# Block-sparse attention and an MLP mixer on one core: the mask product in two pieces, relayouts on VectorE alone, another order of the same work

## The chip, the cores and the metric

The kernel runs on one core of one Trainium2 chip. The metric is the device time of one execution in microseconds (us). A run takes the median of several executions; the profile is of one execution, whose span (first to last instruction) is a little shorter than its time. Engines: PE (TensorE), ACT (ScalarE), DVE (VectorE), POOL (GpSimd) and SP (SyncE), which here issues DMAs and passes on events.

## The reference, cut to what matters

```python
B, H, S, D = 4, 8, 768, 64                        # q, k, v: float32
mask = (|blk_i - blk_j| <= 1) | first or last block row or column
       | three sampled blocks of 32 for each block row
scores = where(mask, q @ k^T / sqrt(D), -1e9)
attn = exp(scores - max) / sum
x = (attn @ v), heads side by side                # [4, 768, 512]
h = relu(x^T @ w_tok1) @ w_tok2                   # token mixer, 768 -> 256 -> 768
u = x + h^T
out = u + relu(u @ w_ch1) @ w_ch2                 # channel mixer, 512 -> 1536 -> 512
```

## The kernel before, in words

All matmuls are bfloat16 with float32 sums in the eight PSUM banks (`banks`). The 32 heads are worked in 16 pairs p. A pair's 768 queries fall into three thirds t, its 768 keys into three pieces jj; a step (p, t, jj) makes the scores of 256 keys by 256 queries for both heads: four matmuls into two banks (`scores`, L917). ACT takes the exponential of the 1,024 columns into the tile `et` of the third (L930). For the first four pairs the mask is part of the scores' matmul (88 rows in place of 64). From pair 4 on (NT0 = 4) the scores use 64 rows, so that the two heads run at once on the two halves of PE's rows, and DVE multiplies `et` by the 0/1 tile `mask` (the function `cut` in `scores`, L948). `CUTS`, chosen by `BASE["cuts"]`, says for which pieces jj one product stands: before, (0, 1, 2) in one operation, which can run when all three exps of the third are done. Then the values product follows (L1086 in full rows for the first pairs, then `pv_halves` by L375), a reciprocal (L1099 and L1040) and a division (L1100 and L1041) into the tile `x`.

Q, K and V come by loads that POOL issues. `relayout` (L757 to L780) copies them into the order that the transposes and the values product take: `klay` and `qlay` (L765) and `vaug` (L762). Before, for pairs from `ra` = 5 on such a copy may go to DVE or ACT. K and Q are transposed by PE for pairs under 8 and by DMA transposes that SP issues from pair 8 on (`crossbar`, L788). The mixer of a batch follows when its four pairs are done: the token mixer (`tok`, `tok_halves`; relus at L1128, L1130, L1218, L1220, additions at L1264, L1326, L1385), the transposes of u (L1145 by SP, L1165 by PE for batch 1) with their evacuations (L1176, L1420, L1449), and the channel mixer `ch` with its relus (L1128 on ACT, L1130 on DVE) and the final addition and store (L1567, L1572 for 1,024 columns; L1615, L1626 for 512).

From pair 4 to the end of the attention PE works in halves (`halves`): each product is split over the two halves of the contraction's rows, so that two matmuls run at once. [...]

The order of the instructions on every engine is fixed when the program is built. A planner (`Planner`) steps through an estimated time. Every piece of work is entered with an estimated cost, with the events it waits for and with a priority; whenever an engine is free in the plan, the ready piece of lowest priority number is emitted next. `P.op` takes work for DVE, ACT or SP; `P.stream` takes PE's work. If a piece may go to two engines, the one that is free first in the plan gets it. The priorities, some limits of PSUM banks (`cps`, `cpo`, `cpm`, `cch`) and some margins (`jit`, `m1`, `m2`, `grace`, `shift`) are read through `KN`: a table `BASE`, and over it `BY_TIME`, which gives other values in numbered stretches of the plan, each 5,000 ns long (`Knobs.stretch`). All costs in these lines are the planner's own, in ns; they decide the order alone.

Of the kernel before, what the change touches and what calls it, by code (L numbers as in the profile page):

```python
# [20 lines left out]
BY_TIME = {  # L21
    0: dict(cch=2),
    1: dict(norm=2.3, m2=300.0, tokp=0.7, ev2=2.0, cch=3),
    2: dict(m2=450.0, ev2=0.9, cpo=1),
    3: dict(norm=2.3, m2=300.0, tokp=0.7, ev2=2.0, cch=3, cpm=3, shift=6000.0, add=0.3, grace=100.0, ev4=1.2),
    5: dict(norm=2.3, m2=150.0, tokp=0.7, ev2=2.0, cch=3, cpm=3, shift=6000.0, add=0.3, grace=100.0, ev4=1.2, cps2=3, relayk=2.0, cut=0.7),
    6: dict(fin=4.1, cps=3, trp=1.6),
    7: dict(fin=4.1, cps=3, trp=1.6),
    8: dict(fin=4.1, cps=3, trp=1.6, add=0.3, back=1.1, cut=0.5),
    9: dict(shift=6000.0),  # L30
    10: dict(fin=4.1, cps=3, trp=1.6, add=0.3, back=1.1, cut=0.5, m2=300.0, ev2=0.9, jit=300.0),
    12: dict(fin=4.1, cps=3, trp=1.6, add=0.3, back=1.1, cut=0.5, m2=300.0, ev2=0.9, jit=300.0, tokp=1.7, backp=0.9, cpo=2, m1=0.0),
    13: dict(fin=4.1, cps=3, trp=1.6, add=0.3, back=1.1, cut=0.5, m2=300.0, ev2=0.9, jit=2000.0, tokp=1.7, backp=0.9, cpo=2, m1=0.0, late=3.5, relayk=0.8),
    14: dict(m2=0.0, cch=2, m1=0.0, cut=6.0, ev4=1.2),
    16: dict(add=0.3, late=1.05, cch=2, ev4=2.0, relayk=3.5),
    17: dict(m1=0.0, back=1.1, add=0.95),
    18: dict(m1=0.0, back=1.1, add=0.95, cut=1.1, m2=300.0, cpo=2),
    19: dict(cps2=3, toks=0.4, jit=300.0, relayv=3.0, relayk=3.5),
    20: dict(m1=0.0, back=1.1, add=0.95, cut=1.1, m2=0.0, cpo=2, toks=-0.5, backp=0.45, cpm=1),
    21: dict(m1=0.0, back=1.1, add=0.95, cut=1.1, m2=0.0, cpo=2, toks=-0.5, backp=0.45, cpm=1),  # L40
    22: dict(m1=100.0, back=1.1, add=0.95, cut=6.0, m2=0.0, cpo=2, toks=-0.5, backp=0.45, cpm=1, relayk=0.8),
    23: dict(m1=100.0, back=1.1, add=0.95, cut=6.0, m2=0.0, cpo=2, toks=-0.5, backp=0.45, cpm=1, relayk=0.8, jit=300.0, cps=3),
    24: dict(m1=100.0, back=1.1, add=0.95, cut=6.0, m2=0.0, cpo=2, toks=-0.5, backp=0.45, cpm=1, relayk=0.8, jit=300.0, cps=3),
    25: dict(jit=450.0, cps2=2, relayv=4.6),
    27: dict(jit=450.0, cps2=2, relayv=4.6, cps=2, backp=0.45, cpo=2, relu=0.85),
    28: dict(jit=450.0, cps2=2, relayv=4.6, cps=2, backp=0.45, cpo=2, relu=0.85),
    29: dict(jit=450.0, cps2=2, relayv=4.6, cps=2, backp=0.45, cpo=2, relu=0.85, toks=0.4, relayk=4.5),
    30: dict(jit=450.0, cps2=2, relayv=4.6, cps=2, backp=0.45, cpo=1, relu=0.85, norm=0.6, cpm=2, backt=0.9),
    31: dict(back=1.1, cpm=1, jit=1300.0),
    32: dict(jit=450.0, cps2=2, relayv=4.6, cps=2, backp=0.45, cpo=1, relu=0.85, norm=1.0, cpm=2, backt=0.9, m1=100.0, shift=0.0),  # L50
    33: dict(tokp=0.7, cps=3, ev4=1.2, shift=-6000.0, cch=2),
    34: dict(chs=0.8, m1=100.0, ev2=1.2, cpo=2, backt=0.2),
    35: dict(jit=0.0, cpo=2, chs=1.1),
}


# [238 lines left out]
def kernel(  # L295
# [12 lines left out]
    nc = tc.nc  # L308
# [7 lines left out]
    NV = 4  # L316
# [15 lines left out]
    vaug = [sb1.tile([128, 2, NC, 66], BF16, name=f"vaug{n}") for n in range(NV)]  # L332
# [32 lines left out]
    def halves(n, cost, outs, lhs, rhs, deps, tags, begin, done, prio, ahead=0.0):  # L365
# [25 lines left out]
        for x in range(n):  # L391
# [11 lines left out]
    P = Planner(  # L403
        {"et": NET, "a_t": 2, "o": 3, "rc": 2, "uT": 2},
# [3 lines left out]
    )  # L408
# [106 lines left out]
    def ind_part(lo, n):  # L515
# [14 lines left out]
        out=ident[:, :], in_=free(one[:, 0:1], 0, [[0, 128]]), compare_op=ALU.is_equal, fill=0.0,  # L530
# [19 lines left out]
    for res, val, lo, hi, op in (  # L550
# [3 lines left out]
            out=res[R, :], in0=val[R, :], scalar1=lo, scalar2=hi, op0=ALU.max, op1=ALU.min  # L554
# [3 lines left out]
        out=bandneg[R, :], in0=notband[R, :], scalar1=inner[R, 0:1], scalar2=MASKVAL,  # L558
# [5 lines left out]
        out=differ[R, :, :], in0=free(kbi[R, 0:1], 0, [[1, 24], [0, 3]]),  # L564
# [188 lines left out]
    def relayout(p):  # L753
        lays = {}
        for nm in ("k", "q", "v") if p >= NT0 else ("v",):
            raw = raws.pop((nm, p))
            arr = arrive.pop((nm, p))  # L757

            def emit(eng, nm=nm, raw=raw):
                copy = nc.scalar.copy if eng == "act" else nc.vector.tensor_copy  # L760
                if nm == "v":
                    copy(out=vaug[p % NV][:, :, :, 0:64], in_=raw)  # L762
                else:
                    lay = sbw.tile([128, NC, 2, D], BF16, tag=f"{nm}lay", bufs=2, name=f"{nm}lay{p}")
# [12 lines left out]
            lays[nm + "ev"] = P.op(("dve", "act") if p >= BASE["ra"] else ("dve",), {"dve": 320.0, "act": 735.0}, deps, emit,  # L777
                                  prio="relayk" if nm != "v" else "relayv")
            copied[nm, p] = lays[nm + "ev"]
        va_there[p] = lays["vev"]  # L780
        return lays

    def crossbar(p):

        lays = relayout(p)
        for nm, bufs, there in (("k", ktb, kT_there), ("q", qtb, qT_there)):
            def emit(eng, nm=nm, bufs=bufs):
                nc.sync.dma_start_transpose(  # L788
                    out=bufs[p % NV][:, 0, :].rearrange("e (c s) -> e c s", c=NC),
                    in_=lays[nm][:, :, :, :].rearrange("p c h d -> p (c h d)"),  # L790
                )
            deps = [lays[nm + "ev"], qk_done[p - NV]]
            ev = P.op(("sp",), {"sp": 1300.0}, deps, emit, prio=1, lat=5000.0)
            there[p, 0], there[p, 1] = ev, ev

    def transposes(p):
# [4 lines left out]
        if p == 0:  # L801
            relayout(p)
            for nm in ("k", "q"):
                copied[nm, p] = Ev(START)
            for hd in range(2):
                kT_there[p, hd], qT_there[p, hd] = k_first[1], q_first[2]
            yield from first_rest()
            return
        for hd in range(2):
            kT_there[p, hd], qT_there[p, hd] = Ev(), Ev()  # L810
        lays = relayout(p)
        for nm, bufs, there in (("k", ktb, kT_there), ("q", qtb, qT_there)):
            box, last, rel = {}, Ev(), Ev()
# [934 lines left out]
```

## Time and profile before

| | |
|---|---|
| median of 3 runs (lowest to highest) | 245.05 us (244.9 to 245.28) |
| profiled execution: time, span | 245.05 us, 243.4 us |
| granted clock of TensorE, mean | 0.999 |
| exps L930 on ACT | 144 of 1,025 ns, 141.6 us |
| mask products L948 on DVE | 36 of 1,703 ns, 61.3 us |
| relayouts L762 and L765 on ACT | 3, of 823, 824 and 833 ns |
| relayouts L762 and L765 on DVE | 37, by form 352 to 476 ns |
| fences L361 | 16 on SP (45.2 to 69.4 us), 73 on POOL (71.1 to 199.5 us) |
| crossbar issues L788 on SP | 16, medians 1.22 and 1.28 us, landing after 2.8 to 4.4 us |
| mixer transposes L1145 on SP | 5, median 1.44 us, landing after 3.7 to 4.7 us |

A group's line in the profile gives the line of the code, the engine, the operation, what it writes and reads with shapes, and the count; then its busy time, the mean time of one, and the idle time of the engine just before, with what ended it. A line of the waits gives who waited, for whom, the time in total, how many times and the longest. Matmuls are pipelined, so that their busy times overlap; the times between their starts tell more.

### The profile page before, as it was taken

How to read it: one execution, taken by the hardware profiler on the slowest of the kernel's cores; microseconds unless marked ns; L12 is line 12 of the kernel's file. 1: busy time of each engine (PE TensorE's matmuls, PEld its weight loads, DVE VectorE, ACT ScalarE, POOL GpSimd, SP SyncE). 2: the span in 40 equal slices, each digit the busy share in tenths (PEclk: the TensorE clock that was granted, in tenths of full speed). 3: DMA queues.
4: the chain of work that ended last, by engine and by line, in shares of the span. 5: the costliest groups of instructions: out<-in, count | busy, mean ns of one | idle time of the engine just before them, and what ended most of it. 6: DMA issues, size and time to landing. Idle time of an engine off the chain costs nothing.

```text
span 243.4 us, 9647 instructions
## 1 busy us (share of the span) xinstructions
PE 237.0 (97%) x4343; PEld 170.9 (70%) x4343; DVE 172.1 (71%) x285; ACT 170.0 (70%) x187; POOL 49.5 (20%) x86
## 2 busy tenths in 40 slices
PE   7999999999999999999999999999999999999994
PEld 3689999767777677867878667677688664565444
DVE  5975987979899889799789788987687535100222
ACT  6889999868797699788778987798658400366000
POOL 8966987357710000000000000000000000000000
PEclk9999999999999999999999999999999999999999
DMA  7999999999993874131207270501030024200132
GB/s 163 166 214 203 209 207 203 206 201 196 201 180 76 132 167 137 38 118 33 40 3 89 46 155 3 154 25 67 3 67 3 5 89 127 112 3 0 43 132 86
DMA packets 39755, 26.17 MB, mean 108 GB/s; under 512 B 21985, under 2 KB 37105, under 8 KB 39713
## 3 DMA queue, kind: packets, MB, share of 16 engines
q0 software_dynamic: 15104, 12.98, 33.9%
q1 hardware_dynamic: 24064, 12.17, 20.4%
q8 instruction: 34, 0.56, 0.9%
q10 hardware_dynamic: 544, 0.39, 0.6%
q14 instruction: 9, 0.07, 0.1%
HBM read 26.74 MB, written 6.29 MB: 136 GB/s over the span
## 4 chain that ended last, share of the span: by engine, by line
PE 89%; DMA 3%; ACT 3%; POOL 2%; DVE 1%; issue 0%; POOLq 0%; DVEq 0%; ACTq 0%
PE banks L375 53%; PE banks L917 14%; PE banks L1601 9%; PE banks L1536 6%; DMA kraw<-in_k_dram 3%; ACT et L930 3%; PE banks L1086 3%; PE banks L858 1%; PE banks L1354 1%; DVE et L948 1%; POOL vraw L447 1%; PE banks L1296 1%; PE banks L1376 1%; PE banks L1318 1%; POOL ktb L517 0%
## 5 line engine op out<-in xcount | busy, mean ns | idle before, releaser
L930 ACT ACTIVATE et<-banks 128x1024 bf16<-128x1024 f32 x144 | 141.6, 1025 | 28.3 <-PE banks L917 24.5
L948 DVE TENSOR_TENSOR et<-et,mask 128x2976 bf16<-128x2976 bf16 x36 | 61.3, 1703 | 8.3 <-ACT et L930 8.2
L917 PE MATMUL banks<-qtb,ktb 64*128 64x256 bf16 (+1 forms) x576 | 63.7, 270 | 0.7 <-ACT et L930 0.2
L375 PE MATMUL banks<-uT,w_ch 64*128 64x512 bf16 (+1 forms) x576 | 60.6, 322 | 0.0
L375 PE MATMUL banks<-w_ch,rc 64*128 64x512 bf16 x384 | 54.3, 376 | 0.0
L375 PEld LDWEIGHTS <-et 64*128 64x128 bf16 x1728 | 39.2, 94 | 9.4 <-POOLq L361 3.0
L917 PEld LDWEIGHTS <-ktb 64*128 64x128 bf16 (+1 forms) x576 | 33.8, 94 | 15.1 <-issue 1.4
L375 PE MATMUL banks<-vaug,et 64*128 64x65 bf16 x1728 | 42.0, 190 | 0.2 <-issue 0.2
L375 PEld LDWEIGHTS <-w_ch 64*128 64x128 bf16 x576 | 28.6, 94 | 8.4 <-SPq L361 0.6
L1128 ACT ACTIVATE rc<-banks 128x512 bf16<-128x512 f32 (+1 forms) x28 | 21.0, 749 | 17.0 <-PE banks L1536 15.0
L1615 DVE TENSOR_TENSOR o<-banks,x 128x512 f32<-128x512 f32 x7 | 4.8, 692 | 28.2 <-PE banks L1601 28.2
L1130 DVE TENSOR_SCALAR rc<-banks 128x1024 bf16<-128x1024 f32 x17 | 20.8, 1221 | 3.4 <-PE banks L375 3.2
L375 PEld LDWEIGHTS <-rc 64*128 64x128 bf16 x384 | 17.3, 94 | 7.9 <-POOLq L361 0.5
L1601 PE MATMUL banks<-w_ch,rc 128*128 128x512 bf16 (+2 forms) x120 | 21.3, 337 | 0.0
L1601 PEld LDWEIGHTS <-rc 128*128 128x128 bf16 x120 | 10.7, 98 | 10.6 <-issue 0.8
L375 PEld LDWEIGHTS <-w_tok 64*128 64x128 bf16 x288 | 14.5, 109 | 3.3 <-POOLq L361 0.6
L1041 DVE TENSOR_TENSOR x<-banks,recip 128x256 bf16<-128x256 f32 x36 | 15.3, 425 | 1.2
L1536 PE MATMUL banks<-uT,w_ch 128*128 128x512 bf16 (+1 forms) x96 | 15.8, 326 | 0.0
L1536 PEld LDWEIGHTS <-w_ch 128*128 128x128 bf16 x96 | 9.4, 98 | 6.4
L1567 DVE TENSOR_TENSOR o<-banks,x 128x1024 f32<-128x1024 f32 x8 | 9.8, 1224 | 5.1 <-PE banks L375 5.0
L1086 PE MATMUL banks<-vaug,et 128*128 128x65 bf16 x288 | 13.1, 193 | 0.0
L1264 DVE TENSOR_TENSOR x<-banks,x 128x512 bf16<-128x512 f32 (+2 forms) x12 | 10.3, 887 | 2.9 <-PE banks L375 2.7
(122 smaller groups left out, 198.0 us busy)
## 6 DMA issues: line engine op xcount, KB each, us to landing
out_dram<-o SPq DMA_DIRECT2D x8, 512.0 KB, 3.6
w_ch<-in_moe_w_ch_dram POOLq DMA_DIRECT2D x8, 384.0 KB, 9.8
vraw<-in_v_dram POOLq DMA_DIRECT2D x10, 192.0 KB, 7.9
out_dram<-o SPq DMA_DIRECT2D x7, 256.0 KB, 2.0
kraw<-in_k_dram POOLq DMA_DIRECT2D x9, 192.0 KB, 9.2
qraw<-in_q_dram POOLq DMA_DIRECT2D x9, 192.0 KB, 8.3
w_tok<-in_moe_w_tok_dram POOLq DMA_DIRECT2D x2, 384.0 KB, 10.0
qf<-in_v_dram POOLq DMA_DIRECT2D x4, 192.0 KB, 7.8
```

Source lines behind the costliest of these rows:

```text
L375: mms.append(nc.tensor.matmul(out=outs()[o](x), lhsT=lhs(o, x, r), rhs=rhs(o, x, r), start=(back == 0 and x == 0), stop=(back == 1 and x = ...
L917: nc.tensor.matmul(out=ps[:, hd, 256 * i : 256 * i + 256], lhsT=ktb[n][rows, h, 256 * jj + 128 * i : 256 * jj + 128 * i + 128], rhs=qtb[n] ...
L930: nc.scalar.activation(out=ets[p, t][:, jj, :, :, :].rearrange("k i h q -> k h i q"), in_=ps.rearrange("k h (i q) -> k h i q", i=2), func= ...
L948: nc.vector.tensor_tensor(out=et, in0=et, in1=free(mask[:, 2 * lo, 256 * t + EDGE : 256 * t + EDGE + 1], 0, [[S, 2 * n], [0, 2], [1, w]]), ...
L1041: nc.vector.tensor_tensor(out=free(xs[b][:, pb // 2, 2 * t, 128 * (pb % 2) : 128 * (pb % 2) + 128], 0, [[64, 2], [256, 2], [1, 64]],), in0 ...
L1086: nc.tensor.matmul(out=po[:, hd, c, :], lhsT=et[:, jj, i, hd, 128 * c : 128 * c + 128], rhs=va[:, hd, 2 * jj + i, 0:65], start=(jj == 0 an ...
L1128: nc.scalar.activation(out=o(), in_=src(), func=AF.Relu)
L1130: nc.vector.tensor_scalar(out=o(), in0=src(), scalar1=0.0, scalar2=None, op0=ALU.max)
L1264: nc.vector.tensor_tensor(out=u, in0=src, in1=u, op=ALU.add)
L1536: nc.tensor.matmul(out=in_bank(pbox["pm"], [k, 128 * n])[:, x // 4, :], lhsT=w_ch1[:, x % 4, 128 * cc : 128 * cc + 128], rhs=st[b]["uT"][: ...
L1567: nc.vector.tensor_tensor(out=t[:, :, :].rearrange("p c (g e) -> p g c e", g=2), in0=free(banks[:, pbox["pm"][0], :], 0, [[256, 2], [512, ...
L1601: nc.tensor.matmul(out=pbox["pm"][:, 0:n], lhsT=box["rc"][:, cc, 128 * sc : 128 * sc + 128], rhs=w_ch2[:, cc, lo : lo + n], start=(cc == 0 ...
```

## The change

`cuts` goes from 2 to 1: a third's mask product becomes two operations, one of the pieces jj = 0 and 1 (8 x 248 = 1,984 elements of each partition) and one of jj = 2 (992). Relayouts may go to DVE alone, and `ra` is gone. The table `BY_TIME` is another one, so that the planner gives another order of the work on PE, DVE, ACT and SP; POOL's loads keep theirs. The stretch length, the code of `crossbar` and all other planned costs are the same in both programs. The core of the diff:

```diff
-    norm=0.6, add=0.3, ev2=1.2, ev4=3.3, grace=0.0, m1=100.0, m2=150.0, nt0=4, cuts=2, xbar=8,
+    norm=0.6, add=0.3, ev2=1.2, ev4=3.3, grace=0.0, m1=100.0, m2=150.0, nt0=4, cuts=1, xbar=8,
...
-    backp=0.45, backt=0.3, turn=[1], ra=5,
+    backp=0.45, backt=0.3, turn=[1],
 }
 BY_TIME = {
-    0: dict(cch=2),
-    1: dict(norm=2.3, m2=300.0, tokp=0.7, ev2=2.0, cch=3),
-    2: dict(m2=450.0, ev2=0.9, cpo=1),
...
-    35: dict(jit=0.0, cpo=2, chs=1.1),
+    1: dict(backt=0.3, chs=1.1, m2=450.0, cpm=3, cps=3),
+    2: dict(relayv=3.0, ev4=2.0, m1=200.0, grace=0.0, fin=0.9),
...
+    35: dict(m1=0.0, shift=1500.0, relayk=6.0, back=0.9, m2=450.0),
 }
...
             def emit(eng, nm=nm, raw=raw):
-                copy = nc.scalar.copy if eng == "act" else nc.vector.tensor_copy
                 if nm == "v":
-                    copy(out=vaug[p % NV][:, :, :, 0:64], in_=raw)
+                    nc.vector.tensor_copy(out=vaug[p % NV][:, :, :, 0:64], in_=raw)
                 else:
                     lay = sbw.tile([128, NC, 2, D], BF16, tag=f"{nm}lay", bufs=2, name=f"{nm}lay{p}")
-                    copy(
+                    nc.vector.tensor_copy(
                         out=lay[:, :, :, :], in_=raw.rearrange("p h c d -> p c h d")
                     )
...
-            lays[nm + "ev"] = P.op(("dve", "act") if p >= BASE["ra"] else ("dve",), {"dve": 320.0, "act": 735.0}, deps, emit,
+            lays[nm + "ev"] = P.op(("dve",), {"dve": 320.0}, deps, emit,
                                   prio="relayk" if nm != "v" else "relayv")
```

What follows from it in the built programs, by counting instructions (before, after): mask products 36 of 2,976, then 36 of 1,984 and 36 of 992; relayouts on ACT 3, then 0, and on DVE 37, then 40; relus of 1,024 columns on DVE (L1130) 17, then 13, and on ACT (L1128) 10, then 14; token relus on DVE (L1220) 3, then 5, and on ACT (L1218) 3, then 1; one evacuation L1420 goes from DVE to ACT; output additions L1567 8, then 7, and L1615 7, then 9; fences 89, then 88. PE's matmuls do the same products, with pair 6's Q turned in halves and a third of batch 2's second channel layer in full rows in place of halves.

More of the change, by code (lines that the diff above doesn't have):

```diff
@@ L20 @@
 )
 BY_TIME = {
-    0: dict(cch=2),
-    1: dict(norm=2.3, m2=300.0, tokp=0.7, ev2=2.0, cch=3),
-    2: dict(m2=450.0, ev2=0.9, cpo=1),
[L25 to L52, printed above, removed]
-    35: dict(jit=0.0, cpo=2, chs=1.1),
+    1: dict(backt=0.3, chs=1.1, m2=450.0, cpm=3, cps=3),
+    2: dict(relayv=3.0, ev4=2.0, m1=200.0, grace=0.0, fin=0.9),
+    3: dict(relayv=3.0, ev4=2.0, m1=200.0, grace=0.0, fin=0.9),
@@ new lines @@
+    4: dict(relayv=3.0, ev4=2.0, m1=200.0, grace=0.0, fin=0.9, cpo=2, cch=2, relu=5.5, add=0.3, trp=0.8),
+    6: dict(relayv=3.0, ev4=2.0, m1=100.0, grace=0.0, fin=0.9, cpo=2, cch=2, relu=5.5, add=0.3, trp=0.8, cpm=2, ev2=1.2),
+    8: dict(relayv=3.0, ev4=2.0, m1=100.0, grace=0.0, fin=0.9, cpo=2, cch=2, relu=5.5, add=0.3, trp=0.8, cpm=2, ev2=1.2, cut=1.1, chs=4.0, relayk=2.0),
+    10: dict(m1=100.0, cpm=2, jit=450.0, cpo=1, late=1.05),
+    11: dict(ev2=1.2, cut=3.2),
+    12: dict(ev2=1.2, cut=3.2),
@@ new lines @@
+    14: dict(backp=0.45, norm=0.6, fin=2.1, backt=0.2, jit=0.0),
+    15: dict(m2=150.0, shift=-1500.0, ev2=2.0, cpm=3, back=1.1),
+    16: dict(m2=150.0, shift=-1500.0, ev2=2.0, cpm=3, back=1.1),
+    17: dict(m2=150.0, shift=-6000.0, ev2=2.0, cpm=3, back=1.1, norm=0.6, m1=200.0, late=9.0, jit=800.0),
+    18: dict(m2=150.0, shift=-6000.0, ev2=2.0, cpm=3, back=1.1, norm=0.6, m1=200.0, late=9.0, jit=800.0, cut=3.2),
+    19: dict(m2=150.0, shift=-6000.0, ev2=2.0, cpm=3, back=1.1, norm=0.6, m1=200.0, late=9.0, jit=800.0, fin=4.1, add=0.3),
@@ new lines @@
+    20: dict(relayk=2.0, norm=0.6, trp=2.6),
+    21: dict(m2=300.0, shift=-6000.0, ev2=2.0, cpm=3, back=1.1, norm=0.6, m1=200.0, late=9.0, jit=800.0, fin=4.1, add=0.3, relu=0.85, cut=5.0, trp=2.0, cch=2),
+    23: dict(jit=450.0, cch=3, tokp=1.5),
+    24: dict(norm=2.3, relayv=1.5, toks=0.4),
+    25: dict(jit=450.0, cch=3, tokp=1.5, relayv=4.6, back=1.1, fin=0.9),
+    28: dict(relayk=6.0, jit=800.0, late=1.05, cut=3.2, backt=0.9),
+    29: dict(cpm=1, relu=0.85),
+    30: dict(back=1.1, toks=0.4, m1=100.0),
@@ L54 @@
+    31: dict(backt=0.3, shift=1500.0, cps=3, cch=1, m1=0.0),
+    32: dict(relayk=0.8, back=0.5, fin=0.9, chs=0.8, trp=2.6),
+    33: dict(backt=0.9, toks=0.4, jit=1300.0),
+    34: dict(backt=0.9, toks=-0.5, jit=1300.0, grace=250.0, back=1.1, cpm=1, trp=1.6),
+    35: dict(m1=0.0, shift=1500.0, relayk=6.0, back=0.9, m2=450.0),
 }
```

## The prediction

> **What bounds the kernel now.** I read the page's first part, then the busy times by stretch, then the chain of work that ended last in order of time, then the waits, and last the rows of the groups that the change touches.
>
> ```profile
> span 243.4 us, 9647 instructions
> ## 1 busy us (share of the span) xinstructions
> PE 237.0 (97%) x4343; PEld 170.9 (70%) x4343; DVE 172.1 (71%) x285; ACT 170.0 (70%) x187; POOL 49.5 (20%) x86
> ```
>
> TensorE carries the span. But matmuls are pipelined, so a busy PE can still lose time, and what the change can move lies in that loss. Its size comes from the starts of the matmuls: 512 columns follow each other in 216 ns, 256 in 109, 128 in 56, 65 in 29, and two matmuls on the two halves of the rows go together, so that each counts half. The last pieces of the chain (start, length, what) confirm the rates:
>
> ```profile
> 208.90 15.60 PE banks L1536 x96
> 224.50 15.61 PE banks L1601 x96
> ```
>
> The first holds 48 matmuls of 512 columns and 48 of 256: 48 x (216 + 109) ns = 15.6 us, so nothing is lost there. At these rates all 4,343 matmuls need 225.7 us; their starts run over 238.9 us. So 13.2 us are lost, and I place them by stretch. Columns: us, then busy us (instructions) of PE, weight loads, DVE, ACT, POOL, then clock and DMA.
>
> ```profile
> 0.00:41.60 41.60, 39.18 (x599) 32.99 (x600) 32.30 (x91) 37.38 (x42) 33.72 (x64) 1.00 1.13 195
> 41.60:51.10 9.50, 9.02 (x218) 6.82 (x216) 8.95 (x18) 7.44 (x10) 4.17 (x7) 1.00 1.26 205
> 51.10:90.40 39.30, 39.11 (x862) 28.52 (x860) 34.48 (x48) 31.89 (x34) 11.64 (x17) 1.00 1.01 163
> 90.40:131.70 41.30, 41.30 (x961) 31.72 (x959) 36.43 (x52) 33.80 (x37) 0.00 (x0) 1.00 0.25 63
> 131.70:172.90 41.20, 41.20 (x918) 29.25 (x914) 34.42 (x43) 35.02 (x36) 0.00 (x0) 1.00 0.34 74
> 172.90:197.30 24.40, 24.38 (x537) 17.81 (x534) 16.50 (x22) 13.11 (x14) 0.00 (x0) 1.00 0.10 22
> 197.30:243.40 46.10, 42.80 (x272) 23.73 (x270) 8.96 (x14) 11.35 (x19) 0.00 (x0) 0.99 0.23 77
> ```
>
> Against the full rate these seven stretches lose 5.6, 2.55, 1.35, 1.2, 1.3, 0.8 and 0.5 us. The granted clock is full throughout, so the losses are waits. The dense part is 41.6 to 197.3 us (7.2 us lost): attention and mixer share PE, DVE is busy 130.8 of 155.7 us and ACT 121.3. Nearly no single long wait of PE is left; what remains is short:
>
> ```profile
> DVE et L948 <- ACT et L930: 8.2, 11, 1.6
> DVE recip L1040 <- PE banks L375: 5.0, 12, 1.2
> ...
> PEld L375 <- POOLq L361: 4.6, 26, 0.3
> ```
>
> The last line is the fence of a half-row group: the second half may start only after POOL (or SP) has seen the first half end. DVE's idle time, 24.9 us in the dense part, is what new DVE work must fit into.
>
> **The change part by part.** The rows used:
>
> ```profile
> L930 ACT ACTIVATE et<-banks 128x1024 bf16<-128x1024 f32 x144 | 141.6, 1025 | 28.3 <-PE banks L917 24.5 <-DVE x L1041 1.6 <-PE banks L375 0.2
> L948 DVE TENSOR_TENSOR et<-et,mask 128x2976 bf16<-128x2976 bf16 x36 | 61.3, 1703 | 8.3 <-ACT et L930 8.2
> L1130 DVE TENSOR_SCALAR rc<-banks 128x1024 bf16<-128x1024 f32 x17 | 20.8, 1221 | 3.4 <-PE banks L375 3.2
> L1264 DVE TENSOR_TENSOR x<-banks,x 128x1024 bf16<-128x1024 f32 x5 | 6.1, 1223 | 2.8 <-PE banks L375 2.7
> L1264 DVE TENSOR_TENSOR x<-banks,x 128x512 bf16<-128x512 f32 x6 | 4.1, 684 | 0.0
> L1128 ACT ACTIVATE rc<-banks 128x1024 bf16<-128x1024 f32 x10 | 10.2, 1023 | 2.0 <-PE banks L375 2.0
> ```
>
> *Mask product in two.* 36 products of 2976 elements become 36 of 1984 and 36 of 992. The elements stay; 36 fixed parts come on top. No row shows the new sizes. The two sizes of L1264 give (1223 - 684)/512 = 1.05 ns per column and 145 ns fixed, so 36 x 0.145 = 5.2 us of DVE. Bounds: nothing, if the first product runs in the 8.2 us that DVE now idles for the third exp; 36 x 0.179 = 6.4 us if each costs a whole smallest instruction (the 128x4 reciprocal, 179 ns). I take 5.2, the nearest row. The second product now waits for the third exp, and behind it on DVE stand norms, relus and adds that free PSUM banks; but after that wait 0.67 us (145 ns + a third of 1.56) remains where 1.70 did.
>
> [...]
>
> *Relayouts.* Three leave ACT (rows 0.82 to 0.83 us, 2.5 us together) for DVE at 0.38, 0.38 and 0.45: 1.2 us.
>
> *The new order.* Counting instructions by form: four relus of 1024 columns move from DVE (-4.9 us) to ACT (+4.1); two first-layer relus of the token mixer move to DVE (+1.1, ACT -1.0), one transpose evacuation to ACT (+0.8, DVE -0.55); one 1024-column output add becomes two of 512 (+0.16). Sum: DVE 5.2 + 1.2 - 4.9 + 1.1 - 0.55 + 0.16 = +2.2 us, ACT +1.4 us, PE -0.14 us. GpSimd's loads keep their order; the last waits for a V relayout placed 4 us of PE work later, but leaves only after 66 us, so that is hidden. On SP one mixer transpose (issue 1.44 us, landing 4.2) now stands before three crossbar issues; the first scores that need them stand 13 us of PE work behind, so I cost it at nothing. Without that cover it would cost its 1.44 us. Despite the change's title the planned crossbar cost (1300 in the code) and the stretch length (5000) are equal in both programs.
>
> *What reaches PE.* For each matmul that waits for an instruction X, which waits for an earlier matmul, I set the PE work that the order puts between the two against X's row plus 0.29 us of hand-over (the shortest exp round trip seen is 1.33 us for a 1.025 us exp; a 17 ns fence takes 0.28 to 0.31). Where the work is less, PE is short by the difference. Sums, before against after, by position in PE's work:
>
> - 2.5 to 35 us: 2.4 against 2.6. I take +0.1.
> - 35 to 42 (the phase switch): 4.25 in 14 places against 4.92 in 16. The trace lost 2.55 there, 0.6 of the sum, so +0.4.
> - 42 to 80: 0.38 against 0.45. +0.1.
> - 80 to 120: 0.70 in 12 places against 2.80 in 20. Five lie within 1.2 us, where batch 1 is turned on PE (a fence short by 0.31, an exp by 0.37, an output add by 0.50, and its evacuations); one stall may pay for several. So between +0.5 and +2.1; I take +1.3.
> - 120 to the end: 1.56 against 0.87. Between -0.7 and 0; I take -0.4.
> - Changes between full-row and half-row matmuls rise from 12 to 16. The 12 lost 1.58 us, with the waits that fell on them; four cost 0 to 0.5. I take +0.2.
>
> [...]
>
> With -0.14 of PE work the sum is -0.14 + 0.1 + 0.4 + 0.1 + 1.3 - 0.4 + 0.2 = +1.56, about +1.5 us. The profiled execution took 245.05 us (span 243.4), which is also the median of the three runs, so **246.5 us**.
>
> **The rivals.**
>
> *DVE becomes the bound.* In the new order the last attention work stands 178.85 us into PE's work, not 183.5, so the dense part holds 144.0 us of PE work instead of 148.5. Minus one output add that moves behind it, DVE has 130.8 + 2.2 - 1.2 = 131.8 us to do in it. My forecast gives that part 144.0 + 7.2 + 1.5 = 152.7 us, so DVE's idle time has to fall from 24.9 to 20.9. If it stayed, 4.0 us would come on top (250.5); if half of the fall fails, **248.5**. For it: DVE is 88% busy at 90 to 132 us already. Against it: the waits for the third exp, 8.2 us, are what the split fills.
>
> *Hidden.* The shortfalls are small, and a stall before one lengthens the distance to the next. If 80 to 120 gives only its least (+0.5) and the later stretches their full -0.7, with no charge for mode changes: -0.14 + 0.1 + 0.4 + 0.1 + 0.5 - 0.7 = +0.26, **245.3**.
>
> *Faster: values products start sooner.* In the trace, waits of PE's values product that involve a mask product lost 1.5 us in 21 places. With the split, its first part needs only two thirds' products, and after the third exp DVE needs 0.67 us instead of 1.70. If that removes 0.9 of the 1.5 and nothing else grows: 245.05 - 0.14 - 0.9 = **244.0**. It decides where DVE is idle when the second exp ends; against it, DVE is 84% busy.
>
> *The change doesn't do what it says*: the products are doubled and the order differs from 9.9 us on, so the programs are not alike; only the crossbar part of the title is empty.
>
> **How the numbers follow.** Forecast case, 245.55 to 247.6: 0.53. DVE bound, above 247.6: 0.18. Hidden, within 0.2% (0.49 us, about what a measurement of this kernel tells from no change): 0.18. Faster: 0.11. The range runs from 244.4, which leaves out most of the faster case, to 249.0, half a us past the middle of the DVE case. Slower 0.53 + 0.18 = 0.71, same 0.18, faster 0.11.
>
> **What would show it.** Right: 36 products near 1.18 us and 36 near 0.67; DVE busy near 174 us, ACT near 171; the first scores-to-tail change about 3 to 4 us earlier than 197.3; losses against full rate of some 2.3 to 2.8 us between 80 and 120 us of PE work. Wrong: a new pair of products at 1.70 us together or less (no fixed part), losses below 1.2 us in that stretch, or DVE idle in the dense part staying at 24 us, which is the DVE rival.

## The result, and the profile after

The changed kernel takes 247.81 us (median of 4 runs, 247.33 to 247.99), the kernel before 245.17 us beside it (4 runs, 244.9 to 245.36). The ratio is 1.0106, 95% interval 1.0088 to 1.0124: slower by 2.6 us where 1.5 was forecast. The profiled execution took 247.99 us. Line numbers of the code are 4 lower than before ahead of `relayout` (L371 was L375) and 5 lower from it on (L943 was L948). The page begins:

```profile
span 246.3 us, 9634 instructions
## 1 busy us (share of the span) xinstructions
PE 238.0 (97%) x4325; PEld 172.6 (70%) x4325; DVE 171.2 (70%) x322; ACT 170.7 (69%) x187; POOL 49.7 (20%) x86
```

The busy times of PE, DVE and ACT are those of before within 1 us: they don't tell where 2.9 us of span came from. The last pieces of the chain are as long as before too, each 1.76 us later:

```profile
210.66 15.60 PE banks L1531 x96
226.26 15.61 PE banks L1596 x96
```

So the loss is ahead of 210 us and behind the last piece. Busy time by stretch (columns as before; cut where the half-row work now ends, 194.3 us):

```profile
41.60:51.10 9.50, 9.21 (x227) 6.95 (x225) 8.63 (x19) 8.80 (x11) 4.39 (x7) 1.00 1.26 207
51.10:90.40 39.30, 38.43 (x830) 28.83 (x826) 32.74 (x55) 31.14 (x32) 12.02 (x17) 1.00 0.98 155
90.40:131.70 41.30, 41.16 (x992) 31.48 (x990) 36.88 (x66) 34.23 (x37) 0.00 (x0) 1.00 0.53 81
131.70:172.90 41.20, 41.19 (x934) 30.66 (x928) 34.99 (x55) 33.75 (x35) 0.00 (x0) 1.00 0.27 65
172.90:194.30 21.40, 21.40 (x490) 16.13 (x482) 15.13 (x25) 13.79 (x14) 0.00 (x0) 1.00 0.11 22
```

In the second of these PE is busy 0.9 of 39.3 us less than the stretch is long; before it was 0.2. DVE is busy 128.4 of the 152.7 us of the five. The two forms of the mask product:

```profile
L943 DVE TENSOR_TENSOR et<-et,mask 128x1984 bf16<-128x1984 bf16 x36 | 42.7, 1187 | 4.0 <-ACT et L925 3.6
L943 DVE TENSOR_TENSOR et<-et,mask 128x992 bf16<-128x992 bf16 x36 | 24.1, 668 | 0.0
```

Together 66.8 us where 61.3 was: 152 ns for each product cut. The waits that answer to those shown of before:

```profile
PEld L371 <- POOLq L357: 4.5, 26, 0.2
...
DVE et L943 <- ACT et L925: 3.6, 8, 0.7
...
PEld L912 <- issue: 2.2, 4, 1.4
```

The fences cost what they did, 4.5 us where 4.6 was, and DVE waits 4.6 us less for exps. (A fence is an empty instruction on SP or POOL, 17 ns in the traces, that waits for the last matmul of a half-row group's first half; PE's second half waits for it.) The third line is new in one respect: before, the longest wait of this kind was 0.3 us. "Issue" means that the profile shows nothing that PE waited for, and here one such wait is 1.4 us long. In the weight loads' order of time it looks so (start, length, idle before):

```profile
57.99 0.10 PEld L371 LDWEIGHTS <-w_ch 64*128 64x128 bf16 x2
59.45 0.11 PEld L912 LDWEIGHTS <-ktb 64*128 64x128 bf16 x3 [1.36 <-issue]
```

The norm on DVE that the matmul behind this load waits for had ended at 58.18 us, 1.27 us before. By the matmuls' starts PE loses 1.14 us here.

Last, the SyncE stores that end the program, four in a row. Before, then after:

```profile
238.21 2.58 SPq L1626 DMA_DIRECT2D out_dram<-o  x4
```

```profile
239.97 3.37 SPq L1621 DMA_DIRECT2D out_dram<-o  x4
```

The third of the four takes 1,318 ns to issue instead of 332 or 333 (the others of this line, in both kernels, 332 to 382), so the last store leaves about 1 us late.

Loss of PE against its full rate, in us, by position in PE's own work, as the prediction counts it; the last column is a second trace of the changed kernel (the last experiment):

| position | before | after | after again |
|---|---|---|---|
| to 35 | 5.57 | 5.81 | 5.33 |
| 35 to 42 | 2.55 | 2.72 | 2.72 |
| 42 to 60 | 0.85 | 1.75 | 1.85 |
| 60 to 80 | 0.50 | 0.48 | 0.48 |
| 80 to 120 | 1.19 | 1.97 | 1.97 |
| 120 to the last matmul | 2.57 | 2.39 | 2.39 |
| last matmul's start to the end of the span | 3.5 | 4.7 | 4.7 |

With 0.14 us less PE work the last matmul starts 1.75 us later than before (again: 1.4), and 1.2 us more is lost behind it. Three items make the result: the standstill at 59 us, the waits between 80 and 120, and the end.

### The profile page after: what moved, and what is told of

It reads as the page before. It is cut to its first block, busy times and chain, and to the rows that moved or that the text cites. A ratio compares the mean times of both kernels' runs of the same rounds, so it can differ in the third digit from the quotient of the medians.

```text
span 246.3 us, 9634 instructions
## 1 busy us (share of the span) xinstructions
PE 238.0 (97%) x4325; PEld 172.6 (70%) x4325; DVE 171.2 (70%) x322; ACT 170.7 (69%) x187; POOL 49.7 (20%) x86
## 4 chain that ended last, share of the span: by engine, by line
PE 90%; ACT 5%; DMA 2%; issue 1%; SPq 0%; DVE 0%; POOLq 0%; DVEq 0%
PE banks L371 51%; PE banks L912 14%; PE banks L1596 11%; PE banks L1531 6%; ACT et L925 4%; PE banks L1081 3%; DMA qf<-in_q_dram 2%; PE banks L853 1%; PE banks L1371 1%; PE banks L1349 1%; PE banks L1313 1%; PE banks L1291 1%; PE banks L818 0%; PE banks L1430 0%; ACT qlay_first L573 0%
## 5 line engine op out<-in xcount | busy, mean ns | idle before, releaser
L943 DVE TENSOR_TENSOR et<-et,mask 128x1984 bf16<-128x1984 bf16 x72 | 65.4, 928 | 4.0 <-ACT et L925 3.6
L371 PE MATMUL banks<-uT,w_ch 64*128 64x512 bf16 (+1 forms) x576 | 61.9, 323 | 0.9 <-issue 0.9
L371 PEld LDWEIGHTS <-et 64*128 64x128 bf16 x1728 | 42.4, 94 | 11.2 <-POOLq L357 3.5
L371 PE MATMUL banks<-w_ch,rc 64*128 64x512 bf16 x336 | 49.0, 376 | 0.0
L371 PE MATMUL banks<-vaug,et 64*128 64x65 bf16 x1728 | 46.0, 190 | 0.2
L1123 ACT ACTIVATE rc<-banks 128x512 bf16<-128x512 f32 (+1 forms) x32 | 25.0, 784 | 19.4 <-PE banks L1531 19.4
L371 PEld LDWEIGHTS <-w_ch 64*128 64x128 bf16 x576 | 27.7, 94 | 7.3 <-POOLq L357 0.7
L1596 PE MATMUL banks<-w_ch,rc 128*128 128x512 bf16 (+2 forms) x144 | 26.5, 344 | 0.0
L1596 PEld LDWEIGHTS <-rc 128*128 128x128 bf16 x144 | 13.1, 98 | 13.4 <-issue 0.8
L1125 DVE TENSOR_SCALAR rc<-banks 128x1024 bf16<-128x1024 f32 x13 | 15.9, 1223 | 7.8 <-PE banks L371 7.6
L371 PEld LDWEIGHTS <-rc 64*128 64x128 bf16 x336 | 15.5, 94 | 5.2 <-issue 0.4
L371 PEld LDWEIGHTS <-w_tok 64*128 64x128 bf16 x288 | 14.9, 109 | 1.8 <-POOLq L357 0.2
L1081 PEld LDWEIGHTS <-et 128*128 128x128 bf16 x288 | 11.7, 97 | 0.5
```

What stands on the lines that cost most here:

```text
L371: mms.append(nc.tensor.matmul(out=outs()[o](x), lhsT=lhs(o, x, r), rhs=rhs(o, x, r), start=(back == 0 and x == 0), stop=(back == 1 and x = ...
L943: nc.vector.tensor_tensor(out=et, in0=et, in1=free(mask[:, 2 * lo, 256 * t + EDGE : 256 * t + EDGE + 1], 0, [[S, 2 * n], [0, 2], [1, w]]), ...
L1081: nc.tensor.matmul(out=po[:, hd, c, :], lhsT=et[:, jj, i, hd, 128 * c : 128 * c + 128], rhs=va[:, hd, 2 * jj + i, 0:65], start=(jj == 0 an ...
L1123: nc.scalar.activation(out=o(), in_=src(), func=AF.Relu)
L1125: nc.vector.tensor_scalar(out=o(), in0=src(), scalar1=0.0, scalar2=None, op0=ALU.max)
L1596: nc.tensor.matmul(out=pbox["pm"][:, 0:n], lhsT=box["rc"][:, cc, 128 * sc : 128 * sc + 128], rhs=w_ch2[:, cc, lo : lo + n], start=(cc == 0 ...
```

## The experiments

The theory formed on these traces, called CODE below, is about PE's own instructions. The trace has an instruction queue of 34 packets of 16 KB in both kernels, for 8,702 PE instructions before and 8,666 after (weight loads, matmuls and a few more): about one packet for 256 instructions. In the changed kernel (packets, MB, share of the DMA engines):

```profile
q8 instruction: 34, 0.56, 1.0%
```

While the loads run, from 45 to 69 us (207 GB/s from 41.6 to 51.1 us), these packets begin about 6 us apart (51.02, 56.98 and 63.14 us in the changed kernel). The standstill ended 1.53 us after one of them had landed. By CODE these packets bring PE's instructions, and PE stands still, with no semaphore to show it, where it works through 256 of them in less time than the next packet takes. The rival of the prediction was that VectorE had become the bound (DVE); the other that only the order and its waits count (ORDER). The first four kernels ran on one chip beside 23 runs of the kernel before (245.06 us).

### Instructions added at the start of the changed kernel

```diff
     for i in range(6):
         idle_mm()
+    for i in range(18):
+        idle_mm(8)
```

> The changed kernel with 18 matmuls of 8 columns more at the start, where PE waits for the first loads; all that follows is in the same order, 36 PE instructions later. In the changed kernel's trace two losses stand beside 16 KB packets of the instruction queue, which come once in about 256 PE instructions: the last but one store's issue on SP takes 1,318 ns in place of 333 beside such a packet at 241.08 us, and PE stands still for 1.14 us at 59.45 us with nothing waited for. Theory of code fetches: the last such packet comes 36 instructions earlier, some 6 us before the end, clear of the stores; SP's last issues take 333 ns again, so about 1 us less (246.8), and the standstill near 59 us goes or moves by 36 instructions. Rival, that both belong to the order of the work: both losses stay and the time stays within 0.3 us of 247.8. If VectorE is the bound, the time stays too.

Measured: 248.13 us, ratio 1.0138 (1.0112 to 1.0165) for the five of six executions that took 247.87 to 249.66 us; the sixth took 253.49 and was not traced. The time was missed. The end went as expected: the last 16 KB packet came at 237.36 us instead of 241.08, no store was slow to issue, and PE's last start stood 3.8 us from the end instead of 4.7. But the standstill did not go:

```profile
59.03 0.20 PEld L914 LDWEIGHTS <-ktb 64*128 64x128 bf16 x4 [1.80 <-issue]
```

This is another instruction of the work: 36 PE instructions earlier, waiting for ACT by its semaphore where the other waited for DVE. Counted from the program's first PE instruction it is the same place. In the changed kernel PE stood still before instruction 1988, here before 1988 as well (991 weight loads stand ahead of it in both; 1.74 us), and 0.36 us before 1732 = 1988 - 256. Nothing of the work is common to these places; the count of PE's instructions is, in steps of 256, each called a block below. What the end gained, the standstills took.

### Less work for VectorE

```diff
-                w = 256 - 2 * EDGE
+                w = 256 - 2 * EDGE - (70 if lo == 2 else 0)
```

> The changed kernel with the product on the third piece cut from 248 to 178 columns of each of its four rows (the last 70 keep unmasked values, so the result is not the reference's): 280 elements less in 36 products, 36 x 0.146 = 5.2 us of VectorE, just what the split added. Same order on every engine. If VectorE is the bound of the dense part: 1 to 2.6 us less, 245.2 to 246.8. If the order of PE's work and the two code fetches make the loss: within 0.4 us of the changed kernel, 247.4 to 247.8.

Measured: 248.53 us (246.76 to 249.35, six executions), ratio 1.013 (1.0097 to 1.0163), above both expectations. The second products fell from 668 to 521 ns:

```profile
L943 DVE TENSOR_TENSOR et<-et,mask 128x712 bf16<-128x712 bf16 x36 | 18.8, 521 | 0.0
```

5.3 us of DVE work less, and no time gained by the median. The traced execution is the shortest of the six; what it takes less than the changed kernel's lies before 20 us, at the standstill and behind the last matmul. PE's loss at 80 to 120 us of its work is 1.97 us as in the changed kernel, and it stands still before instruction 1988 for 1.04 us. DVE is not what PE waits for. Why the other executions spread up to 249.35 us is not shown.

### The products split in the old order

```diff
-                et = free(ets[p, t][:, lo, 0, 0, EDGE : EDGE + 1], 0, [[512, 2 * n], [256, 2], [1, w]])
-                nc.vector.tensor_tensor(
+                for a, m in ((0, 2), (2, 1)):
+                    et = free(ets[p, t][:, a, 0, 0, EDGE : EDGE + 1], 0, [[512, 2 * m], [256, 2], [1, w]])
+                    nc.vector.tensor_tensor(
```

> The kernel before, with each mask product written as two operations (1,984 and 992 elements) one behind the other at the place of the one; PE, ACT and SP keep their order. VectorE has 36 fixed parts more, 5.2 us by the rows. If VectorE's load is what slows the changed kernel: 1 to 2.6 us more, 246.2 to 247.8. If the order does: at most 0.5 us more, 245.2 to 245.7, since the values product has 3.5 us and more of PE work between its scores and itself.

Measured: 244.93 us (12 runs), ratio 0.9999 (0.9986 to 1.0011), with the products' rows as in the changed kernel:

```profile
L949 DVE TENSOR_TENSOR et<-et,mask 128x1984 bf16<-128x1984 bf16 x36 | 42.6, 1184 | 0.9 <-ACT et L930 0.9
L949 DVE TENSOR_TENSOR et<-et,mask 128x992 bf16<-128x992 bf16 x36 | 24.1, 670 | 0.5 <-ACT et L930 0.5
```

The split alone costs nothing that can be measured. What the changed kernel loses comes with its order. The DVE rival falls with these two.

### Lighter loads, in the changed kernel and in the one before

```diff
             nc.gpsimd.dma_start(
                 out=raw,
                 in_=APx(src, 2 * p * S * D, [[NC * D, 128], [S * D, 2], [1, NC * D]]),
+            ) if p not in (8, 9, 10, 12, 13, 15) else nc.gpsimd.dma_start(
+                out=raw[0:16],
+                in_=APx(src, 2 * p * S * D, [[NC * D, 16], [S * D, 2], [1, NC * D]]),
             )
```

> The changed kernel with the loads of pairs 8, 9, 10, 12, 13 and 15 cut to the first 16 of 128 partitions (old values stand in the rest, so the result is not the reference's); the order is the same on every engine. From 47 to 66 us the queues carry far less. Theory that a code fetch that queues behind the loads makes PE's standstill of 1.14 us at 59.45 us: fetches between 45 and 70 us come sooner than every 6 us, the standstill goes, and the time falls by about 1.1 us to 246.7. Rival, that it is a wait of the order: the standstill stays and the time is within 0.3 us of 247.8.

> The kernel before, with the loads of pairs 8, 9, 10, 12, 13 and 15 cut to 16 of their 128 partitions (it leaves that data out, as the light loads of the changed kernel did, which took 1.7 us off it). CODE theory: what the light loads took off the changed kernel is its standstill of 1.14 us at PE instruction 1988, 1.5 us behind a 16 KB packet of the instruction queue; before has only 0.36 us of that kind (at instruction 1732), so it gains 0.3 to 0.5 us: 244.6 us. LOADS rival: lighter transfers help this kernel whatever the order, through earlier data or less contention: it gains 1.7 us as the changed kernel did, 243.4 us, and then light loads say nothing of the change.

Measured: the changed kernel 246.07 us, ratio 1.0043 (1.0024 to 1.0062), where unedited it stands at 1.0106; the kernel before 244.46 us, ratio 0.9976 (0.9953 to 0.9998). So lighter loads take some 1.5 us off the one and 0.6 off the other, near the 0.3 to 0.5 expected for the latter and not the 1.7 of the LOADS rival. In the traces the packets in question landed 2.3 and 2.8 us before PE came to instructions 1732 and 1988 of the changed kernel, and neither kernel stands still at any such place (before: its 0.36 us at 1732 is gone). They also exclude a rival for the standstill: the semaphore of the matmul at 1988 is updated by a relu on DVE as well, which in the changed kernel ended at 59.31 us, 0.14 us before PE went on. With light loads PE passes that matmul at 58.05 us, 0.90 us before the relu ends, so it does not wait for the relu. The losses at 42 to 60 are 0.39 and 0.50 us, those at 80 to 120 stay at 1.97 and 1.20. The standstill of the changed kernel therefore belongs to the loads and to the place in PE's code together, and the loss at 80 to 120 belongs to neither.

### The edges of the blocks moved without touching the order

Idle matmuls at the start, where PE waits for data anyway, move the blocks against the work. By the spacing of the starts, and 6 us for a block under loads, a shift by 60 instructions should hurt the kernel before most, and one by 200 should help the changed kernel.

```diff
-    for i in range(6):
+    for i in range(4):
         idle_mm()
+    for i in range(32):
+        idle_mm(8)
```

> The kernel before with two of its six idle products of 512 columns at the start replaced by 32 of 8 columns: 60 PE instructions more, the same 2.6 us of PE; nothing else is touched. CODE theory: the same reckoning with about 6.0 us per block of 256 makes this about the worst place for the edges in the kernel before: standstills of about 2 us at PE instructions 1732 and 2244, in place of 0.4: 246.6 us (245.9 to 247.0). ORDER rival: the order of the work is that of before, so the time is too: 245.1 us.

Measured: eight of twelve executions took 245.39 to 246.45 us (median 245.9), ratio 1.0028 (1.0003 to 1.0053), the other four 249.95 to 250.81; none of those four was traced, but the next kernel shows a likely reason. The trace:

```profile
63.61 0.11 PEld L375 LDWEIGHTS <-w_ch 64*128 64x128 bf16 x2
64.98 0.31 PEld L375 LDWEIGHTS <-w_ch 64*128 64x128 bf16 x5 [1.26 <-issue]
```

This is before instruction 2244 = 1988 + 256, one of the two places named; PE loses 1.09 us there, where the kernel before loses nothing. The other place, 1732, shows none, since the packet ahead of it landed at 51.58 us and not, as before, at 52.22; so the size was half of the forecast. The time alone would not show it: instruction for instruction, the traced execution is 0.55 us later than that of the kernel before already at 20 us, with two long products fewer at the start (next kernel), and two other traces of the old order (split in place, light loads) are 0.48 and 0.64 us earlier there. From 60 to 66 us, where instruction 2244 lies, it loses another 1.25 us against that kernel. The order of the work is that of the kernel before, instruction by instruction, so ORDER falls as the cause of such standstills.

```diff
-    for i in range(6):
-        idle_mm()
+    for i in range(106):
+        idle_mm(8)
```

> The changed kernel with its six idle products of 512 columns at the start replaced by 106 of 8 columns: 200 PE instructions more, about the same 2.6 us of PE before the first data. CODE theory: blocks of 256 PE instructions now begin 200 instructions earlier in the work, where PE takes longer over each block of the loading stage; from the starts of the changed kernel and about 6.0 us that a block needs there from one edge to the next, the standstills in 42 to 70 us fall from 1.3 to about 0.6 us, and the last 16 KB packet no longer lies beside the last stores (1 us of the profiled run): 246.3 us, and nothing stands still at the instruction that stood still before. ORDER rival: the loss belongs to the order of the work and to its waits, and instructions added at the start are nothing or a loss: 247.8 us or more.

Measured: 246.81, 247.02, 247.33 and 247.82 us in four executions (ratio 1.0081, 1.0044 to 1.0117), and 251.4 to 254.3 in eight. The time decides nothing for CODE: the idle products of 512 columns turned out to have a use. In the traced execution (one of the eight) PE does a third of the matmuls in the same time, shown first; the changed kernel second:

```profile
10.00:15.00 5.00, 5.00 (x29) 1.00 1.16 179
```

```profile
10.00:15.00 5.00, 5.00 (x84) 1.00 1.22 191
```

Matmuls of 256 columns follow each other in 213 ns until 21.9 us, then in 109; in the changed kernel that change comes at 4.5 us, and with four of the six long products kept, at 9.0 us. At 19 us of the changed kernel the same instructions come 6.8 us later here, and everything behind lies later against the loads. The clock column says 1.00 throughout. One sign of CODE did come: the work that stood still in the changed kernel does not here, and standstills lie before instructions 2244 and 2756; but with the loads shifted this is no clean trial.

Where PE waits for ACT or DVE, it goes on about 50 ns after the end of the instruction that it waited for (medians of 52 to 54 ns, over the waits of more than 100 ns, in the traces of before and after). The table has the standstills of over 0.45 us, in all traces of this study between 25 and 190 us, at which that instruction had ended 0.5 us or more before, or at which there was nothing to wait for; all other standstills of that size end within 0.1 us of an update of a semaphore that PE waits for:

| kernel | PE instruction | packet landed, us | PE went on, us | between | PE lost |
|---|---|---|---|---|---|
| changed | 1988 | 57.92 | 59.45 | 1.53 | 1.14 |
| changed, again | 1988 | 57.53 | 59.08 | 1.55 | 1.14 |
| changed, 36 added | 1988 | 57.51 | 59.04 | 1.53 | 1.74 |
| changed, less DVE work | 1988 | 57.24 | 58.76 | 1.52 | 1.04 |
| changed, 200 added | 2244 | 66.17 | 67.39 | 1.22 | 0.47 |
| changed, 200 added | 2756 | 78.31 | 79.77 | 1.46 | 0.57 |
| before, split in place | 2500 | 69.98 | 71.34 | 1.36 | 0.50 |
| before, 60 added | 2244 | 63.75 | 64.98 | 1.23 | 1.09 |
| before, new table | 1988 | 58.37 | 59.75 | 1.38 | 0.49 |
| before, new table | 2244 | 64.42 | 65.94 | 1.52 | 1.54 |

Each index is 196 plus a multiple of 256. And in no trace does PE pass such an index between 1476 and 2500 less than 1.2 us after the packet has landed that began in the block before (up to 3.8 us after PE had passed that block's first instruction). So these traces show the place of a standstill and its condition; what happens in those 1.2 to 1.55 us they do not show.

### One part of the change alone, re-planned

The changed kernel with the table of before:

```diff
 BY_TIME = {
-    1: dict(backt=0.3, chs=1.1, m2=450.0, cpm=3, cps=3),
...
+    0: dict(cch=2),
+    1: dict(norm=2.3, m2=300.0, tokp=0.7, ev2=2.0, cch=3),
...
```

> The changed kernel's code (whole products split in two, relayouts on VectorE alone) with the numbers by time of the kernel before, so the order is planned anew from the old table. It tells the new table from the rest. CODE theory: PE comes to instruction 1988 0.9 us sooner in its own work than before, and the blocks of the loading stage cost about 0.9 us more than in before (1.96 by the reckoning with 6.0 us per block, against 1.09 by the same reckoning for before): 245.9 us. VectorE rival (its 5.5 us more of products decide): 246.5 us or more. TABLE rival (only the new numbers by time cost anything): 245.1 us.

The kernel before with the products cut in the plan:

```diff
-    norm=0.6, add=0.3, ev2=1.2, ev4=3.3, grace=0.0, m1=100.0, m2=150.0, nt0=4, cuts=2, xbar=8,
+    norm=0.6, add=0.3, ev2=1.2, ev4=3.3, grace=0.0, m1=100.0, m2=150.0, nt0=4, cuts=1, xbar=8,
```

> The kernel before with each whole product planned as two operations (thirds two and one), everything re-planned from the old numbers by time; relayouts stay free to go to ScalarE. The same two operations put in place without a new plan cost nothing (244.93 us), and the changed code with the old numbers took 253.3. SPLIT-PLAN theory: the two operations, as the planner prices them, are what moves the order, and 7 to 8 us of those 8 come with this edit alone: 252 to 253 us. RELAYOUT rival: the relayouts on VectorE alone are the cause: here 245 to 246 us. BOTH rival: only the two together upset the plan: 246 to 249 us.

The kernel before with no relayout left to ACT:

```diff
-    backp=0.45, backt=0.3, turn=[1], ra=5,
+    backp=0.45, backt=0.3, turn=[1], ra=99,
```

> The kernel before with all relayouts planned on VectorE, re-planned from the old numbers by time; products stay whole. SPLIT-PLAN theory: three relayouts of 2.5 us in all leave ScalarE, nothing else: 245.1 us (244.8 to 245.6). RELAYOUT rival: the order is upset by this: 252 us or so. In the loading stage its PE instructions lie as in before, so no new standstill there by the CODE theory.

The kernel before with the new table (the first diff of these, turned round, and nothing else):

> The kernel before with the new numbers by time, so the old operations in an order planned from the new table. CODE theory: its PE comes to instructions 1988, 2244 and 2500 after 48.3, 52.7 and 58.3 us of its own work (before: 50.5, 56.1, 61.4), which at about 6.0 us per block in the loading stage costs 4.2 us against 1.1 by the same reckoning for before: 248.2 us, with standstills at indices 1732 to 2244. If PE's code is no limit: what remains is the planner's mismatch, of unknown size, with no standstill at these indices.

Measured:

| code | table | us | ratio to before | PE lost at 42 to 80, 80 to 120, 120 to the end |
|---|---|---|---|---|
| before | old | 245.1 | 1 | 1.35, 1.19, 2.57 |
| new | old | 253.34 | 1.0326 (1.0288 to 1.0365) | 2.71, 5.41, 4.71 |
| split alone | old | 254.82 | 1.0405 (1.0381 to 1.0429) | 2.60, 6.85, 4.52 |
| relayouts alone | old | 249.08 | 1.0163 (1.0145 to 1.0182) | 1.60, 1.99, 5.79 |
| before | new | 253.79 | 1.0361 (1.0336 to 1.0386) | 6.26, 2.69, 3.18 |
| new | new | 247.81 | 1.0106 (1.0088 to 1.0124) | 2.23, 1.97, 2.39 |

None of the three theories for the first had this: 253.3 is far over CODE and TABLE, and the VectorE rival, whose "246.5 us or more" has no upper end, gave no reason for 8 us. The split alone takes 1.8 us more than its first theory (252 to 253), relayouts alone cost 4 us where 0 was expected, and the two together cost less than the split. So the parts don't add up: each row off the pairs old with old and new with new costs 4 to 10 us, whichever part is exchanged. A likely reading, not shown, is that the numbers by time fit one set of operations and prices: with any part exchanged the planner emits another order. With the split re-planned, ACT is busy 177.6 us (170.0 before), and DVE's wait for exps doubles from 8.2 us:

```profile
DVE et L948 <- ACT et L930: 16.1, 18, 2.1
```

With the old code and the new table, waits without a releaser rise, as CODE foretold for this kernel, at the indices 1988 and 2244 (see the table of standstills):

```profile
PEld L371 <- POOLq L357: 6.6, 33, 0.4
...
PEld L371 <- issue: 4.6, 12, 1.5
...
PEld L913 <- issue: 3.2, 8, 0.9
```

These standstills are 2.0 us of its 4.9 us more at 42 to 80; its total was missed by 5.6 us, since the rest is ordinary waits. In the first of the four, nothing stood still at these indices, against the 0.9 us that CODE expected.

### The changed kernel once more

> The changed kernel once more, nothing edited, for a second trace of it. CODE theory: the standstill at PE instruction 1988 is set by the order and the loads, so it is there again, 1.0 to 1.3 us, 1.5 us behind the end of a 16 KB packet; the slow issue of the second-last store (1,318 ns where all others take 332) hangs on where the last such packet falls to within a microsecond, so it may be absent, and then this run is about 0.9 us shorter from PE's last start to the end (3.8 us, not 4.7). Rival: both are accidents of one execution: no standstill, and a time about 1.1 us lower. Time 247.0 to 248.0 us by the first, 246.7 or less by the second.

Measured: 247.67 us (246.91 to 248.47), ratio 1.0109 (1.0069 to 1.015). The second trace repeats the first to the hundredth from 60 us of PE's work to the last matmul (table of losses above), with 1.14 us before instruction 1988 again, and the slow store as well, which the expectation took for a possible accident:

```profile
239.59 3.40 SPq L1621 DMA_DIRECT2D out_dram<-o  x4
```

The issue took 1,346 ns, from 241.17 us, beside a 16 KB packet at 240.58 to 242.14 us. In the kernel with less DVE work and in that with light loads, which have as many PE instructions, the last packet came after the last store's issue (245.78 and 244.31 us) and all four issues took 332 or 333 ns; with 36 instructions added it came before them all, likewise. But the packet alone does not explain it. In the traces of this study 35 other stores of the result were issued while such a packet was moving, among them the store just ahead of the slow one in both traces, and each took 332 to 375 ns. So the slow issue is seen in both traces of the changed kernel and in no other kernel, and its cause stays open.

## Why the prediction was right or wrong, point by point

The direction was right, the time lies in the range, and the size was short by 1.1 us. By the steps of the prediction:

- **Mask product in two**, +5.2 us of DVE: measured 5.5, 152 ns for each product cut where 145 was taken. That these 5 us cost PE nothing by themselves is shown by the split in place (ratio 0.9999) and by the kernel with less DVE work.
- **DVE's total**, +2.2: the durations sum to +1.9 (182.4 to 184.3 us), but the profile's busy time fell by 0.9. In 16 of the 24 back-to-back pairs the second product begins 82 to 85 ns before the recorded end of the first, and the profile's busy time counts that once.
- **The full rate**: at the rates as stated, with half of 29 ns for a half-row matmul of 65 columns (14.5; the median step is 15.0), the 4,343 matmuls need 227.4 us and not 225.7, which takes 13.5 ns. The table of losses above counts as the prediction does. At 14.5 ns its differences from 35 us on are +0.2, +0.9, +0.2, +0.5 and 0.0, so the standstill keeps its size and the part at 80 to 120 shrinks. Not all of the loss is waiting, either: the clock column is full, but until 3.1 us the trace of before has 427 ns from one product of 512 columns to the next where 216 is the full rate.
- **DVE becomes the bound**: fell. Yet the sign that the prediction gave for it appeared: DVE is idle 24.3 of 152.7 us between 41.6 and 194.3 us, not under 21. The sign was bad, because busy time shrinks by that overlap; the length of the part, forecast as 152.7 us from 41.6 us on, was right (the first full-row matmul after it starts at 194.47).
- **35 to 42**, +0.4, and +0.2 for mode changes: +0.17 together.
- **42 to 80**, +0.1: this step failed. It measured +0.88 (+0.98 in the second trace). The step compares the PE work between an instruction and what it waits for with the durations on the other engines. It has no term for the packets of the instruction queue, and the 1.14 us standstill lies 1.53 us behind one of them, with nothing else to wait for; the kernel before paid 0.36 us of the same kind, at 1732.
- **80 to 120**, +1.3 between 0.5 and 2.1: +0.78, in both traces (about +0.5 at 14.5 ns, the low end of the range), unmoved by lighter loads or by less DVE work. The largest single piece is where it was put: a fence 0.285 us late at 93.5, then two of 0.065 us at 94.0 and 94.7. The rest is waits for exps on ACT at 108.8 (0.23) and 113.8 (0.12) and for fences. The mechanism held, with one stall paying for several, and the size was too large by 0.5.
- **120 to the end**, -0.4: -0.18.
- **The sum for PE**, +1.56: the last matmul starts 1.75 us later in the first trace and 1.4 in the second. This agreement is partly luck: 0.8 us too little at 42 to 80 stands against 0.5 and 0.4 too much at 80 to 120 and 35 to 42.
- **Behind the last matmul**: forecast nothing, measured +1.2 us, of which the slow issue of a store is 1.0. This is the second step that failed, as large as the shortfall against the result. The prediction followed SP's queue for the mixer transposes only. Why that issue is slow stays open.
- **Hidden** (245.3) and **Faster** (244.0): both fell. Values products did start without waiting as long (DVE's waits for exps fell from 8.2 to 3.6 us), but PE's time is not made there.

That a packet holds 256 of PE's instructions is the reading of two counts: 34 packets for 8,702 and 8,666 instructions, and standstills a multiple of 256 apart. At most of these places PE loses nothing of the standstills' size; while the loads ran at about 200 GB/s it lost 1.14 us at one of them in the changed kernel, and up to 1.74 with 36 instructions added.

What stays open: why exactly these four waits at 80 to 120 grew (they are of the new order; no kernel changed that order there alone), and what makes the store's issue slow. No kernel of this study beats the one before; the only time clearly below it, 244.46 us, leaves loads out.

## What to carry to other kernels

When PE stands still for "issue" with its semaphores long signalled, count its instructions from the start of the program: here the places were a multiple of 256 apart, each 1.22 to 1.55 us behind the landing of a 16 KB packet, in a stage in which the loads ran at about 200 GB/s and the packets came about 6 us apart, and lighter loads took the standstill away. A planner's fitted numbers and the operations it plans are one thing: judge an edit by the same order first (the split in place cost nothing), and then the new order for itself. Compare the queue of the last stores as well as the busy engines: here one slow issue there cost 1.0 us that no busy share shows.

## What the runs showed of the hardware that I had not expected

- Under loads (about 200 GB/s) the packets of the instruction queue came 5.9 to 6.2 us apart in the changed kernel, and between instructions 1476 and 2500 PE passed a block's edge no sooner than 1.2 us after the packet had landed; the standstills ended 1.22 to 1.55 us after.
- One store's issue on SP, the third of the last four, took 1,318 and 1,346 ns in the two traces of the changed kernel. All 35 other stores issued beside a packet of the instruction queue took 332 to 375.
- Without the six idle products of 512 columns PE ran at half its rate (213 ns for 256 columns, 109 later) until 21.9 us, with no idle time in the two stretches from 10 to 20 us, while the profile's clock column showed 1.00; with them it came to full rate at 4.5 us, 3.5 us after its first matmul. What brought the change, and why it came so late with short products, no trace here shows.
